# Sliding-window attention and a gated convolution FFN on one core: loading q and k through GpSimd's DMA queue with a cast on the way

## The chip, the core and the metric

The kernel runs on one core of a Trainium2 chip. The core has five engines that run side by side, each in its own instruction order: TensorE (PE, matrix products into PSUM), VectorE (DVE), ScalarE (ACT), GpSimd (POOL) and SyncE (SP, which here only issues transfers). Sixteen DMA engines move data between HBM and the on-chip memory SBUF; an issuing engine hands them work through its queue. The metric is the device time of one execution in microseconds. The kernel before took 213.82 us (median of 3 runs, 212.24 to 214.0).

## The reference, cut to what matters

Shapes: q, k and v are (8, 8, 576, 64) in fp32, that is batch, heads, sequence and head size; w_in is 512 x 1024, conv_w is 3 x 1024 and w_out is 1024 x 512.

```python
scores = q @ k.T / 8                            # per batch and head
scores = where(abs(i - j) <= 32, scores, -1e9)  # window of 32 to both sides
attn   = softmax(scores)
x      = concat_heads(attn @ v)                 # (8, 576, 512)
h      = maximum(x @ w_in, 0)                   # (8, 576, 1024)
conv   = conv_w[0]*h[s-1] + conv_w[1]*h[s] + conv_w[2]*h[s+1]
out    = (h * sigmoid(conv)) @ w_out            # (8, 576, 512)
```

The output is fp32. The kernel works in bf16 between the products.

## The kernel before, in words

**The order is written out by hand or by a planner.** The string `ORDER` (line 15) lists 869 steps as short words. A loop at line 654 calls one function per word, and each engine keeps exactly that order: an instruction that waits holds back all that stands behind it on its engine. `lq,1,0` is "load q of batch 1, head group 0"; a letter at the end names the engine (`a` ACT, `d` DVE, `p` POOL), and `@5` a PSUM bank. Since all instructions go through one helper (line 164), the profile gives line 164 for nearly all of them, and they are told apart by their tiles.

**Attention.** A batch has two units of four heads (G = 0, 1). For each unit, q and k (4 heads x 576 rows x 256 bytes, 576 KiB each) are loaded in fp32 into a staging tile `st` (`lq`, `lk`, line 194, SP's queue), cast to bf16 into `qb` by ACT or POOL (`cq`, `ck`, line 202), and transposed in blocks by DVE into `qT`, `kT` (`tq`, `tk`, line 206). A partition of `st` holds 18 consecutive rows of a head. For batch 0 each load, cast and transpose is made in two parts, which are the first nine and the last nine of the 18 rows of every partition, so a part is spread over the whole sequence and both are needed for any score.

Scores are made in two halves of the sequence (`sc`: h = 0 has the 64-row tiles 0 to 3, h = 1 the tiles 4 to 8; the keys of a tile reach 32 rows to both sides, so the first half needs q rows up to 256 and k rows up to 288), then the exponential (`ex`, ACT), the band mask (`mk`, DVE or POOL), the product with v and the row sums (`av`, PE), and the division (`nr`, DVE). v comes in five blocks of 128 rows per batch (`lv`, SP, 256-byte pieces) into `vst`, and is cast into `ve` (`cv`) and, shifted by 64 rows, into `vo` (`vo` by POOL from `vst` or by DVE from `ve`; `vd` copies it by DMA). The result x is transposed by PE and ACT (`xp`, `xe`) or by a DMA (`xt`).

**FFN.** Two batches together are cut into three chunks of 384 rows; the first two chunks are halved, which gives 14 pieces. For a piece, `ph` multiplies by w_in (PE, 256 channels at a time), `re` applies the relu (ACT), the convolution runs in one of several ways (`pc`, `tp`: `P` full diagonal matrices on PE, `A` and `D` quarter-array diagonal matrices on PE, `X` on ACT and DVE, `G` on POOL), `th` is the tanh that stands for the sigmoid (ACT), `ga` the gating (DVE), `py` multiplies by w_out (PE), `ye` moves it out of PSUM (ACT or DVE) and `st` stores it (SP). w_in and w_out come in four quarters of 512 KiB each (`li`, `lo`, SP's queue), and are cast by ACT or POOL (`ci`, `co`).

In the order before, SP issues at first the eight parts of q and k of batch 0, the five blocks of v, then k of unit (1,0), two quarters of w_in, q of (1,0), the two other quarters, and so on.

Of the kernel before, what the change touches and what calls it, by code (L numbers as in the profile page):

```python
# [10 lines left out]
U32 = mybir.dt.uint32  # L11
# [4 lines left out]
lk,0,0,0 lq,0,0,0 s3 s1 lq,0,0,1 lk,0,1,1 s2 lk,0,1,0 lk,0,0,1 cw@5 lq,0,1,1 lq,0,1,0 cc lv,0,2 dg,1,a dg,0,d lv,0,1  # L16
dg,2,d cq,0,0,0,a cq,0,0,1,p dg,7,a ck,0,1,1,p dg,4,a s4 tq,0,0,1 dg,5,a tk,0,1,1 ck,0,0,0,p dg,3,a s5 tq,0,0,0 s0
ck,0,1,0,a s7 tk,0,0,0 lv,0,3 ck,0,0,1,p tk,0,0,1 cq,0,1,1,a tk,0,1,0 sc,0,0,1@4 tq,0,1,1 cq,0,1,0,p sc,0,0,0@0
ex,0,0,1 lv,0,4 tq,0,1,0 cv,0,2,p lv,0,0 ex,0,0,0 mk,0,0,1,d sc,0,1,1@4 lk,1,0 ex,0,1,1 cv,0,1,p li,1 vo,0,1,d li,3
sc,0,1,0@4 mk,0,0,0,d lq,1,0 cv,0,3,a li,0 mk,0,1,1,d li,2 cv,0,4,a vo,0,2,d vo,0,3,d cv,0,0,a lq,1,1 ex,0,1,0  # L20
vo,0,0,d lk,1,1 av,0,0,0@0 mk,0,1,0,d lv,1,2 ck,1,0,a nr,0,0,0 av,0,1,0@3 nr,0,1,0 av,0,0,1@0 ci,1,a xp,0,1@6 nr,0,0,1
dg,6,a xp,0,0@2 xe,0,1,a ci,3,p av,0,1,1@4 xe,0,0,a nr,0,1,1 ph,0,3@3 lv,1,1 cq,1,0,p tk,1,0 xp,0,2@7 re,0,3 xp,0,4@5
xp,0,3@4 xe,0,2,a ph,0,1@0 xe,0,3,a tq,1,0 pc,0,3,P@6 ci,0,p re,0,1 ph,1,3@4 th,0,3,P xe,0,4,a ga,0,3,P sc,1,0,0@0
re,1,3 ph,0,0@5 ci,2,p ex,1,0,0 lv,1,0 pc,1,3,P@7 re,0,0 ph,2,0@4 mk,1,0,0,d th,1,3,P cq,1,1,p sc,1,0,1@0 ph,2,2@5
ex,1,0,1 ph,2,3@6 tq,1,1 re,2,2 ck,1,1,p lv,1,4 ph,2,1@3 ga,1,3,P ph,1,0@5 re,2,1 lv,1,3 tk,1,1 cv,1,2,p re,2,0
ph,1,1@0 re,1,0 re,1,1 mk,1,0,1,d lo,1 sc,1,1,0@1 cv,1,1,p lo,2 pc,0,1,P@5 ex,1,1,0 ph,0,2@7 cv,1,0,p vo,1,1,d re,2,3
sc,1,1,1@0 re,0,2 ph,1,2@4 vo,1,0,d ex,1,1,1 mk,1,1,0,d lv,2,1 av,1,0,0@6 lo,0 re,1,2 nr,1,0,0 cv,1,3,p av,1,1,0@0
lk,2,1 cv,1,4,a pc,1,0,P@2 lo,3 nr,1,1,0 pc,1,2,P@4 vo,1,3,p th,1,0,P lv,2,0 pc,0,0,P@7 th,0,1,P ga,1,0,P th,1,2,P
xp,1,0@3 mk,1,1,1,d xp,1,1@6 co,1,p xe,1,0,a pc,1,1,P@1 lq,2,1 xe,1,1,a ga,1,2,P pc,0,2,P@2 lk,2,0 ga,0,1,P pc,2,0,X@0
ph,3,2@3 vo,1,2,p th,1,1,P tp,2,0,X ph,3,0@4 re,3,2 th,0,2,P ph,3,1@6 re,3,0 lv,2,2 pc,3,2,G ga,0,2,P pc,2,3,P@5  # L30
th,0,0,P ga,1,1,P re,3,1 av,1,0,1@3 co,0,a ga,0,0,P av,1,1,1@1 nr,1,0,1 pc,2,2,P@6 lq,2,0 co,2,a pc,2,1,P@7 ck,2,1,p
nr,1,1,1 lv,2,3 ph,3,3@3 th,2,0,X th,2,3,P pc,3,0,P@4 re,3,3 co,3,p ga,2,3,P xp,1,4@1 th,2,1,P xp,1,3@2 pc,3,1,P@3
th,3,0,P ga,2,1,P cv,2,0,p pc,3,3,P@5 xe,1,4,a ga,2,0,X th,2,2,P xp,1,2@1 cv,2,1,p th,3,1,P py,0,1@7 ga,2,2,P vo,2,0,p
ga,3,1,P cq,2,1,a s6 tk,2,1 lv,2,4 py,0,2@6 tp,3,2,G xe,1,2,a tq,2,1 th,3,3,P xe,1,3,a lq,3,0 ga,3,0,P lk,3,0
sc,2,1,0@0 ga,3,3,P ck,2,0,p py,1,0@4 ex,2,1,0 ye,0,1,d cv,2,2,p th,3,2,G@5 lk,3,1 tk,2,0 ye,0,2,a vo,2,1,p sc,2,1,1@0
lv,3,0 cq,2,0,a ga,3,2,G ph,4,3@6 ye,1,0,d ex,2,1,1 lv,3,1 tq,2,0 cv,2,3,p py,0,0@4 vo,2,2,p re,4,3 mk,2,1,0,d lk,4,0
cv,2,4,a mk,2,1,1,d sc,2,0,1@0 ye,0,0,a vo,2,3,p av,2,1,0@6 ex,2,0,1 ph,4,2@4 nr,2,1,0 st,0,0 mk,2,0,1,d sc,2,0,0@0
# [24 lines left out]
st,5,1 tk,6,0 th,8,2,A ph,9,0@2 mk,5,0,1,d re,9,1 ga,8,2,A av,5,1,1@4 re,9,0 av,5,0,1@0 nr,5,1,1 pc,9,1,D@6 cq,6,1,a
# [24 lines left out]
def kernel(  # L87
# [22 lines left out]
    PAD = 32  # L110
# [71 lines left out]
    def slot(y, b, G):  # L182
        return 2 * unit(b, G) + y
# [507 lines left out]
```

## Time and profile before

| | |
|---|---|
| time, median of 3 runs | 213.82 us (212.24 to 214.0) |
| time of the profiled execution | 214.61 us |
| its span, first to last instruction | 212.9 us |
| busy: PE, DVE, ACT, POOL | 188.9, 178.5, 173.0, 147.7 us |
| DMA: bytes, mean rate over the span | 46.90 MB, 220 GB/s |
| mean granted TensorE clock | 0.998 |

A busy share is a mean over the whole span, and stages differ, so the tables by stage and the chain of work that ended last say more than the totals. In the groups by shape, a row gives the engine, the operation, output<-input by tile names, the shapes, the count, then the busy time in us, the mean ns of one, and the idle time of the engine ahead of them with what ended it. "DMA share" is the mean busy share of the 16 DMA engines; it can read a little over 1.

### The profile page before, as it was taken

The page shows a single profiled execution, that of the slowest core. Times are in us where ns is not written, and L with a number is a line of the kernel's source. Part 1 is how long each engine was busy: PE and PEld are TensorE (multiplying, and loading weights), DVE is VectorE, ACT ScalarE, POOL GpSimd, SP SyncE. Part 2 cuts the span into 40 slices and gives each one's busy share as a digit, 9 for nine tenths or more (in the row PEclk, how much of TensorE's full clock was granted, in tenths as well). Part 3 has the DMA queues.
Part 4 walks back from the last instruction along what each step waited for, and adds up shares of the span by engine and source line. Part 5 has one row for each costly group of instructions (what it writes and reads, how often), then busy time and mean ns, then how long its engine had stood idle before and what let it go on. Part 6 is the DMA issues. An engine that isn't in the chain of part 4 may idle for free.

```text
span 212.9 us, 7087 instructions
## 1 busy us (share of the span) xinstructions
PE 188.9 (89%) x2936; PEld 113.4 (53%) x2936; DVE 178.5 (84%) x297; ACT 173.0 (81%) x265; POOL 147.7 (69%) x177
## 2 busy tenths in 40 slices
PE   1035899999999799999999999999899997999994
PEld 0034899986566355644464554544555553545443
DVE  4689839999999999798999779898899487889860
ACT  2987778998899799789999699887989797759911
POOL 2630686379999569999799999497723979855700
PEclk9999999999999999999999999999999999999999
DMA  5999999999896794899999899979985664132225
GB/s 171 333 202 345 390 246 304 353 327 283 243 262 177 193 316 144 261 299 229 251 280 157 209 280 233 309 248 183 271 202 130 89 153 127 29 86 99 98 102 197
DMA packets 66165, 46.90 MB, mean 220 GB/s; under 512 B 53180, under 2 KB 55508, under 8 KB 66132
## 3 DMA queue, kind: packets, MB, share of 16 engines
q1 hardware_dynamic: 66096, 46.43, 83.0%
q8 instruction: 23, 0.38, 0.8%
q14 instruction: 10, 0.08, 0.2%
q10 hardware_dynamic: 36, 0.01, 0.1%
HBM read 32.52 MB, written 9.44 MB: 197 GB/s over the span
## 4 chain that ended last, share of the span: by engine, by line
PE 64%; DVE 13%; ACT 7%; SPq 6%; DMA 5%; issue 3%; ACTq 0%; DVEq 0%
PE PS L164 64%; SPq L164 6%; DVE gT L164 3%; DMA xT<-in_moe_w_in_dram 3%; DVE attn L164 2%; DVE xn L164 2%; DVE qT L164 2%; DVE PS L164 2%; ACT PS L164 2%; DMA xT<-xn 2%; ACT hT L164 1%; ACT attn L164 1%; ACT y L164 1%; ACT xT L164 1%; DVE rec L164 1%
## 5 line engine op out<-in xcount | busy, mean ns | idle before, releaser
L164 PE MATMUL PS<-xT,w_in_sb 128*128 128x385 bf16 (+3 forms) x448 | 70.7, 309 | 3.0 <-ACT y L164 1.3
L164 PE MATMUL PS<-w_out_sb,gT 128*128 128x512 bf16 (+1 forms) x296 | 66.7, 374 | 0.0
L164 DVE SCALAR_TENSOR_TENSOR gT<-PS,hT 128x384 bf16<-128x384 f32 (+2 forms) x82 | 52.6, 650 | 6.0 <-ACT PS L164 4.9
L164 PEld LDWEIGHTS <-w_in_sb 128*128 128x128 bf16 x448 | 41.4, 100 | 25.8 <-issue 5.6
L164 ACT ACTIVATE hT<-PS 128x770 bf16<-128x770 f32 (+3 forms) x56 | 39.9, 721 | 11.9 <-PE PS L164 9.5
L164 PEld LDWEIGHTS <-gT 128*128 128x128 bf16 x296 | 27.6, 98 | 30.2 <-issue 1.2
L164 ACT ACTIVATE attn<-PS 128x1280 bf16<-128x1280 f32 (+1 forms) x32 | 36.0, 1132 | 4.6 <-PE PS L164 4.1
L164 POOL TENSOR_TENSOR zg<-zg,tap 128x768 f32<-128x768 f32 (+1 forms) x18 | 31.8, 1764 | 1.5
L164 ACT ACTIVATE PS<-PS 128x768 f32<-128x768 f32 (+1 forms) x47 | 30.0, 652 | 3.0 <-PE PS L164 2.2
L164 PE MATMUL PS<-hT,diag_w 64*64 64x384 bf16 (+2 forms) x354 | 27.5, 311 | 0.1
L164 DVE TENSOR_TENSOR xn<-PS,rec 128x512 bf16<-128x512 f32 (+1 forms) x32 | 26.4, 824 | 1.1
L164 PE MATMUL PS<-qT,kT 32*128 32x64 bf16 x1152 | 15.3, 195 | 11.5 <-DVE kT L164 7.9
L164 POOL TENSOR_SCALAR ve<-vst 128x512 bf16<-128x512 f32 x24 | 16.8, 708 | 12.4 <-DMA vst<-in_v_dram 11.9
L164 DVE TENSOR_TENSOR attn<-attn,mask 128x1280 bf16<-128x1280 bf16 (+1 forms) x24 | 22.9, 959 | 2.1 <-ACT attn L164 1.9
L164 POOL TENSOR_SCALAR vo<-vst 64x512 bf16<-64x512 f32 x32 | 22.7, 708 | 2.5
L164 POOL TENSOR_SCALAR_AFFINE_SELECT attn<-attn 64x1024 bf16<-64x1024 bf16 (+1 forms) x16 | 19.7, 1234 | 6.7 <-ACT attn L164 6.0
L164 DVE STREAM_TRANSPOSE qT<-qb 128x576 uint32<-128x576 uint32 (+1 forms) x18 | 20.2, 1128 | 4.1 <-POOL qb L164 2.1
L164 POOL TENSOR_SCALAR qb<-st 128x1152 bf16<-128x1152 f32 (+1 forms) x18 | 18.9, 1054 | 6.7 <-DMA st<-in_q_dram 5.6
L164 PEld LDWEIGHTS <-kT 32*128 32x128 bf16 x1152 | 11.9, 96 | 21.2 <-issue 9.6
L164 ACT CAST qb<-st 128x1152 bf16<-128x1152 f32 (+1 forms) x18 | 19.1, 1073 | 2.0 <-DMA st<-in_q_dram 1.2
L164 POOL TENSOR_SCALAR tap<-hT,conv_w_sb 128x384 f32<-128x384 bf16 (+1 forms) x36 | 20.1, 571 | 0.9
L164 DVE STREAM_TRANSPOSE kT<-qb 128x576 uint32<-128x576 uint32 (+1 forms) x18 | 19.9, 1124 | 0.9 <-PE PS L164 0.8
(47 smaller groups left out, 195.7 us busy)
## 6 DMA issues: line engine op xcount, KB each, us to landing
out_dram<-y SPq DMA_DIRECT2D x35, 256.0 KB, 4.1
st<-in_k_dram SPq DMA_DIRECT2D x14, 576.0 KB, 6.2
st<-in_q_dram SPq DMA_DIRECT2D x14, 576.0 KB, 5.8
vst<-in_v_dram SPq DMA_DIRECT2D x24, 256.0 KB, 6.6
vst<-in_v_dram SPq DMA_DIRECT2D x16, 192.0 KB, 5.5
st<-in_k_dram SPq DMA_DIRECT2D x4, 288.0 KB, 5.3
st<-in_q_dram SPq DMA_DIRECT2D x4, 288.0 KB, 4.9
vo<-ve SPq DMA_DIRECT2D x8, 130.0 KB, 4.2
```

The source lines that it names most:

```text
L164: return lambda *args, **kwargs: tc.keep_in_program_order(do(*args, **kwargs))
```

## The change

- New steps `gq`, `gk` issue loads of q and k from GpSimd's queue straight into the bf16 tile `qb`; the transfer casts. They replace load and cast of all of batch 0 (eight loads, in parts) and of 22 of the 28 later loads (whole). The six others, q and k of unit (1,0), k of (3,0), k of (4,1) and k of (7,0) and (7,1), stay with SP and their casts with ACT (2) and POOL (4).
- The parts of batch 0 are now stretches of the sequence: q rows 0 to 255 and 256 to 575, k rows 0 to 287 and 288 to 575. The source of a part is 4 heads x 32 pieces of 8 to 10 rows.
- There are 5 tiles `st` instead of 6 and 6 tiles `qb` instead of 4.
- The whole order is new. SP now begins with the blocks of v, then two quarters of w_in, q and k of unit (1,0), and the two other quarters. Beside that, 5 mask products move from POOL to DVE, 7 evictions `ye` from DVE to ACT, 7 casts of v from POOL to ACT, 4 `vo` from DVE to POOL, 2 casts of w_out from ACT to POOL; one block of x is transposed by PE instead of by a DMA; of the convolutions, 15 instead of 19 are of kind `P`, and none of these is full-width (before: 5), 9 instead of 7 `A` and 15 instead of 13 `D`. Functions `gi`, `go` are added and not called.

The start of the order, and the functions:

```diff
-lk,0,0,0 lq,0,0,0 s3 s1 lq,0,0,1 lk,0,1,1 s2 lk,0,1,0 lk,0,0,1 cw@5 lq,0,1,1 lq,0,1,0 cc lv,0,2 dg,1,a dg,0,d lv,0,1
...
+gk,0,0,0 s5 s4 tk,0,0,0 s3 lv,0,1 lv,0,2 gq,0,0,0 lv,0,4 s1 lv,0,0 cw@1 gk,0,1,0 s0 lv,0,3 gq,0,1,0 cc s2 gq,0,0,1
+cv,0,2,a tq,0,0,0 gk,0,0,1 cv,0,1,a li,0 s7 sc,0,0,0@0 dg,5,a vo,0,1,p li,1 ex,0,0,0 tk,0,1,0 lq,1,0 lk,1,0 gk,0,1,1
+cv,0,0,a tq,0,1,0 li,2 gq,0,1,1 mk,0,0,0,d sc,0,1,0@0 li,3 vo,0,0,p ex,0,1,0 tq,0,0,1 dg,0,a mk,0,1,0,d cv,0,3,p
+cv,0,4,a tk,0,0,1 av,0,1,0@4 dg,3,a av,0,0,0@6 vo,0,3,p dg,1,a nr,0,1,0 lv,1,1 sc,0,0,1@0 nr,0,0,0 ex,0,0,1 vo,0,2,p
+tk,0,1,1 xp,0,0@7 tq,0,1,1 xp,0,1@6 xe,0,0,a ci,0,p mk,0,0,1,d xe,0,1,a sc,0,1,1@2 ex,0,1,1 gk,1,1 lv,1,0 av,0,0,1@0
+ci,1,a mk,0,1,1,d ph,0,0@5 nr,0,0,1 cq,1,0,p av,0,1,1@6 re,0,0 dg,2,a ph,0,1@3 nr,0,1,1 gq,1,1 re,0,1 ck,1,0,p tq,1,0
+xp,0,3@2 xp,0,2@6 xe,0,3,a pc,0,1,P@0 xe,0,2,a tk,1,0 xp,0,4@7 xe,0,4,a ph,1,1@1 ci,2,p tk,1,1 sc,1,0,1@2 re,1,1
...
-    NST, NQB, NQT, NAT, NY = 6, 4, 3, 4, 4
+    NST, NQB, NQT, NAT, NY = 5, 6, 3, 4, 4
...
+    def part_of(y, part):
+        if not part:
+            return 0, RP
+        first = (256, 288)[y] // 32
+        return (0, first) if part[0] == 0 else (32 * first, RP - first)
+
+    def columns(t, t0, g):
+        return t[:, 2 * t0:2 * t0 + D * g]
+
+    def rows(y, b, G, *part):
+        t0, g = part_of(y, part)
+        src = (q, k)[y][b, 4 * G:4 * G + 4, t0:t0 + 32 * g, :]
+        heads = [[S * D, 4], [g * D, 32]] if part else [[g * D, 128]]
+        return bass.AP(src.tensor, src.offset, heads + [[1, g * D]])
+
+    def load_qk(y, b, G):
+        sync.dma_start(st_[slot(y, b, G) % NST], rows(y, b, G))
+
+    def fetch_qk(y, b, G, *part):
+        gpsimd.dma_start(columns(qb_[slot(y, b, G) % NQB], *part_of(y, part)), rows(y, b, G, *part))
+
+    def cast_qk(y, b, G, e):
+        copy(e, qb_[slot(y, b, G) % NQB], st_[slot(y, b, G) % NST])
+
+    def turn_qk(y, b, G, *part):
+        t0, g = part_of(y, part)
+        src = columns(qb_[slot(y, b, G) % NQB], t0, g).bitcast(U32).rearrange("p (g d) -> p g d", g=g)
+        to = qT_[unit(b, G) % NQT] if y == 0 else kT_[unit(b, G) % NQT][:, PAD:PAD + S, :]
+        to = to[:, t0:t0 + 32 * g, :].rearrange("p s e -> p (s e)").bitcast(U32)
+        vector.transpose(to.rearrange("p (x g) -> p g x", g=g), src)
...
+        gq=lambda *a: fetch_qk(0, *a), gk=lambda *a: fetch_qk(1, *a),
```

More of the change, by code (lines that the diff above doesn't have):

```diff
@@ L21 @@
[L21 to L25, printed above, removed]
```

167 lines of the change are left out of this document (71 added, 96 removed).

## The prediction

> **What bounds the kernel now.** I read the page's summary first, then the table of stages, then the chain of waits in order of time, then the groups by shape.
>
> ```profile
> span 212.9 us, 7087 instructions
> PE 188.9 (89%) x2936; PEld 113.4 (53%) x2936; DVE 178.5 (84%) x297; ACT 173.0 (81%) x265; POOL 147.7 (69%) x177
> PE 64%; DVE 13%; ACT 7%; SPq 6%; DMA 5%; issue 3%; ACTq 0%; DVEq 0%
> ```
>
> TensorE is busy for 188.9 of 212.9 us and owns 64% of the chain that ended last. So 24.0 us is idle time of PE, and the question is where it lies.
>
> ```profile
> core 0: us, PE busy (x) PEld busy (x) DVE busy (x) ACT busy (x) POOL busy (x), PEclk, DMA share, GB/s
> 0.00:2.00 2.00, 0.00 (x0) 0.00 (x0) 0.57 (x8) 0.00 (x0) 0.71 (x6) 1.00 0.13 12
> 2.00:11.00 9.00, 0.59 (x2) 0.50 (x2) 5.16 (x19) 6.92 (x19) 4.11 (x8) 1.00 0.96 305
> 11.00:16.00 5.00, 2.13 (x133) 1.92 (x137) 4.46 (x8) 4.16 (x5) 1.92 (x3) 1.00 0.95 200
> 16.00:23.60 7.60, 4.48 (x116) 3.84 (x104) 6.66 (x17) 6.30 (x11) 1.05 (x1) 1.00 1.01 354
> 23.60:32.00 8.40, 8.38 (x142) 7.73 (x142) 5.07 (x6) 5.27 (x11) 6.84 (x7) 1.00 1.11 302
> 32.00:53.00 21.00, 20.40 (x344) 17.53 (x342) 20.00 (x36) 19.49 (x39) 14.54 (x22) 1.00 1.12 316
> 53.00:138.00 85.00, 83.59 (x1356) 45.00 (x1356) 77.83 (x114) 75.04 (x101) 73.01 (x83) 1.00 0.97 240
> 138.00:181.00 43.00, 40.52 (x655) 21.93 (x650) 35.76 (x57) 36.43 (x52) 30.95 (x34) 1.00 0.76 177
> 181.00:202.00 21.00, 21.00 (x189) 10.84 (x184) 18.92 (x33) 17.26 (x29) 14.56 (x17) 1.00 0.25 79
> 202.00:213.00 11.00, 7.85 (x45) 4.12 (x42) 4.08 (x6) 2.08 (x4) 0.00 (x0) 0.96 0.38 145
> ```
>
> Before 23.6 us PE is busy for 0.59+2.13+4.48 = 7.2 us, idle for 16.4. From 32 to 202 it is idle for only 0.60+1.41+2.48 = 4.5 us in 170, and at the end for 3.15. From 23.6 on, PE's own work sets the pace; what can be won is in the start. There the DMA share is 0.95 to 1.01 from 2 us on: the first 23.6 us are bound by transfers.
>
> ```profile
> 13.72 6.94 DMA xT<-in_moe_w_in_dram
> ...
> 20.69 1.05 ACT w_in_sb L164
> ...
> 23.62 11.51 PE PS L164 x170
> ```
>
> The chain says the same: a quarter of w_in lands at 20.66, ACT casts it, and the first FFN matmul runs at 23.62.
>
> **The change part by part.** The rows that carry its costs:
>
> ```profile
> L164 PE MATMUL PS<-hT,diag_w 64*64 64x384 bf16 x240 | 13.3, 330 | 0.0
> L164 PE MATMUL PS<-hT,diag_w 128*128 128x192 bf16 x84 | 8.8, 251 | 0.0
> L164 PE MATMUL PS<-hT,diag_w 128*128 128x384 bf16 x30 | 5.6, 326 | 0.1
> L164 POOL TENSOR_SCALAR vo<-vst 64x512 bf16<-64x512 f32 x32 | 22.7, 708 | 2.5
> L164 POOL TENSOR_SCALAR ve<-vst 128x512 bf16<-128x512 f32 x24 | 16.8, 708 | 12.4 <-DMA vst<-in_v_dram 11.9
> L164 POOL TENSOR_SCALAR qb<-st 128x1152 bf16<-128x1152 f32 x13 | 15.6, 1200 | 1.6 <-DMA st<-in_q_dram 0.9 <-DMA st<-in_k_dram 0.3
> L164 ACT CAST qb<-st 128x1152 bf16<-128x1152 f32 x15 | 17.2, 1156 | 2.0 <-DMA st<-in_q_dram 1.2 <-DMA st<-in_k_dram 0.8
> L164 DVE COPY vo<-ve 64x520 bf16<-64x520 bf16 x16 | 5.8, 362 | 0.2
> L164 ACT CAST ve<-vst 128x512 bf16<-128x512 f32 x16 | 9.8, 620 | 0.2 <-DMA vst<-in_v_dram 0.2
> L164 ACT COPY y<-PS 128x512 f32<-128x512 f32 x23 | 13.2, 586 | 6.8 <-PE PS L164 6.3 <-DMA out_dram<-y 0.4
> L164 POOL TENSOR_SCALAR_AFFINE_SELECT attn<-attn 64x1024 bf16<-64x1024 bf16 (+1 forms) x16 | 19.7, 1234 | 6.7 <-ACT attn L164 6.0
> L164 POOL MEMSET vst<- 32x512 f32 x2 | 1.0, 518 | 0.1
> L164 POOL TENSOR_SCALAR w_in_sb<-hT 128x1024 bf16<-128x1024 f32 x1 | 1.1, 1053 | 8.1 <-DMA hT<-in_moe_w_in_dram 8.1
> L164 DVE STREAM_TRANSPOSE kT<-qb 128x288 uint32<-128x288 uint32 x4 | 2.7, 708 | 0.1
> L164 SPq DMA_DIRECT2D st<-in_k_dram x18: 328/500/1056, 0.8 to 148.0; - x18
> L164 SPq DMA_DIRECT2D vst<-in_v_dram x40: 367/540/4158, 5.2 to 168.1; - x40
> DMA to landing us min/median/max: 2.9/5.8/10.6
> ```
>
> *Price of a GpSimd issue, e.* No row has one. SP issues the same q, k loads in 0.33 to 1.06 us, median 0.50, and a v load in up to 4.16: those are the ends. I take 0.9, about twice SP's median, since POOL needs 708 ns for a half of vo that DVE copies in 362. Below nothing I exclude: the issue is an added instruction. The Trainium skill ("DMA: Bandwidth & Descriptors", Specifications) gives about 1 us to the first byte on GpSimd's path against 0.6 on SP's; with 1.0 the sum below ends 0.8 us later.
>
> *The transfers of the start.* Before, SP moved in this order: q, k of batch 0 (eight loads of 288 KiB, 2.36 MB), v (1.18 MB), k of one unit of batch 1 (0.59), the w_in quarter that the chain waits for (0.52). At the stage rates that is 2.0 + 2.36/0.305 + 1.18/0.200 + (0.59+0.52)/0.354 = 2.0+7.7+5.9+3.1 = 18.7 us, 2.0 below the 20.66 at which it landed; I add that 2.0 as the landing. After, q, k go by GpSimd's queue and SP holds v, then two w_in quarters, then q, k of batch 1. Both queues draw on the same engines, whose share is already full, so I let them add: 2.0+7.7+5.9 = 15.6 for q, k and v together, and the first quarter 1.5 later, 17.1, landed by 19.1. I assume that a cast on the way moves source bytes at the rate of a plain load. From above: only half the bytes are written, up to 3.9 us less. From below: half the rate, 7.7 us more.
>
> *POOL's chain at the start*, in its order: eight issues; identity and mask, for which I allow 0.8 (the first 2 us hold 0.71 of POOL work); zero rows 1.0; four vo steps of 2 x 0.708; one v cast 0.71; the w_in cast 1.05: 9.2 us without the issues, 16.4 with 8 x 0.9, so from 0.8 done by 17.2 when nothing is late. Something is: the last v block comes with the end of q, k, v at 15.6, and behind it stand cv 0.71, two vo 2.83 and ci 1.05, so 20.2. PE's first FFN product stands there: 20.2 against 23.62.
>
> *DVE's chain* starts when the first part lands (0.8 and the least landing of 2.9, so about 4). All DVE work before 23.6 us is 16.9 by the stage table, with eight halves of vo that POOL now makes (2.9); the eight part transposes (0.71 each) and what stands between them can be no more than the other 14.0, so the last is done by 18: hidden, with 2 us to spare at least. A part is now a stretch of the sequence, so the first half's scores need only part 0. The new wait here is DVE's mask set-up behind the first transpose; POOL's mask step and its fifth issue queue behind that, and POOL comes to it at 0.8 + 4 x 0.9 + 1.3 = 5.7 anyway, after the transpose's 4.7.
>
> *Unit (1,0)* stays with SP and is late next. Its k is behind 2.36+1.18+1.05+1.18 MB: 2.0+7.7+5.9+3.0+3.3 = 21.9. Its casts stand on POOL behind ci, with an issue ahead of each (0.9+1.2+0.9+1.2), so 24.4, a transpose of 1.25, and PE's scores at 25.7. Two w_in casts queue behind (26.5). PE reaches these scores after three FFN products, the transposes of x and one convolution, exactly what stands ahead of the same scores before:
>
> ```profile
> 23.62 1.45 PE L164 MATMUL PS<-xT,w_in_sb 128*128 128x193 bf16 x8 [0.62 <-ACT xT L164]
> ...
> 28.81 0.42 PE L164 MATMUL PS<-qT,kT 32*128 32x64 bf16 x32
> ```
>
> 28.81-23.62 = 5.2 us, so 25.4 against 25.7. The start is worth 28.81-25.7 = **-3.1 us**. Bounds: -5 (cast at a better rate, e = 0.5) to +6 (below).
>
> *Conversions.* ACT and POOL lose 18 casts each and keep 2 and 4, 16.8 and about 14 us; ACT takes 7 v casts (620 ns) and 7 y evictions (586 ns), POOL 4 vo steps from DVE, DVE 5 mask products from POOL. POOL ends at 147.7-14.1+5.7-5.0+2.1-12.3 = 124 us plus 30 issues, 151 with e = 0.9. Neither sets the end, so the gain is nothing directly; PE is the cover.
>
> *Convolutions.* Five full-width pieces on diagonal matmuls (5.6/5 = 1.12 us of PE) become four on quarter tiles (13.3/20 = 0.67) and one more half piece (0.63): -2.3 us of PE. One more transpose of x (four products, against six in a half piece of 0.63) gives up to 0.5 back. DVE pays with two or three shorter gates in place of one, so I count half of the 1.8: **-0.9**.
>
> *Middle.* PE is idle for 4.5 us between 32 and 202. Lighter ACT may take some; a load that lands at 10.6 instead of the median 5.8 gives 4.8 back, and POOL's order now holds loads between its conversions: if one waits for a qb slot, the vo, cv and convolution taps behind it wait, and with them PE. Slots are six for four per batch, so I expect them free. **0**, from -4 to +9.
>
> Sum: -3.1-0.9 = -4.0: span 208.9. The profiled execution took 214.61 us with 212.9 of span, 0.8 above the median 213.82; on the median, **209.8 us**.
>
> **Rivals.**
> *A, given back (chance 0.20, about 213).* PE starts earlier, but batch 1's loads, now on two queues, come no earlier: the DMA share stays at 1.1 to 53 us, and a middle worse by 3 takes the rest. For it: the full share; against: only 0.6 us of idle PE from 32 to 53.
>
> *B, POOL's issues (0.22, 219.4).* POOL's 9.2 us and 8e, from 0.8 on, must fit before 23.62: with e over 1.7 POOL's w_in cast ends later than the start of before. At e = 2.2 it ends at 27.6, +4.0; POOL's total is 124+66 = 190, as much as PE, and in-order conversions cost perhaps 2.5 more: 213.8+4.0+2.5-0.9 = 219.4. For it: v loads that took SP 4.16. Against: SP's median of 0.50.
>
> *C, few engines for the parts (0.06, 219.4).* Their source has 4 heads outermost. If a part runs on four of 16 engines, it moves at 354/4 = 88 GB/s, 3.3 us a part. On rotating groups the first lands 2.4 later, which DVE's 2 us nearly cover. On the same four, all eight need 2.36/0.088 = 26.8 us: PE starts at about 30.1, +6.5, and 213.8+6.5-0.9 = 219.4. The Trainium skill ("DMA: Bandwidth & Descriptors", Why a DMA increments its semaphore by 16 and not by 1) states that the engines used are the largest number up to 16 that divides the slowest dimension of both sides, here 4, with rotating groups on GpSimd's path; it also notes direct copies there that take all 16. No row of before has such a load.
>
> *D, the cast is slow (0.06, 226).* At half rate q, k take 15.4 us: the start goes +4.3 against before; 22 loads add 1.67 us of all engines each, 37 in all, where the share is near 1. A quarter of that uncovered gives 213.8+4.3+9-0.9 = 226.
>
> *That it brings more (0.08, 205).* Start -5, middle -3.
>
> **How the numbers follow.** Forecast 0.38, from 207 to 211.6. About 1% (2.1 us) is what can be told from no change. Faster: 0.38+0.08 = 0.46. Within 1%: A, 0.20. Slower: B, C, D, 0.34. The range runs from 205.5, leaving out half of the last rival, to 221.5, leaving out D and the worse part of B: 0.82 held.
>
> **What would show it.** In the changed kernel PE's first product of xT with w_in starts near 20 us (right), or after 23.6 (wrong, then the row just before names POOL or a landing). The distance of POOL's early instructions gives e: about 0.9. The landing of q, k on GpSimd's queue beside 5.8 us, and the GB/s from 2 to 16 us, show a slow cast or few engines (below 200). PE's idle time from 32 to 202 stays near 4.5. POOL's total is near 150. The prediction fails if e exceeds 1.7, if the cast lowers the rate, or if PE meets late q, k after 53 us.

## The result and the profile after

The changed kernel takes **228.68 us** (median of 4 runs, 227.02 to 229.18) against 213.33 for the kernel before beside it: a ratio of 1.0711, 95% interval 1.0634 to 1.0789. The prediction was 209.8, from 205.5 to 221.5, and faster. The profiled execution took 229.13 us. Medians here are over all runs, while the ratios leave out executions more than 1.5% above the fastest of their kernel, so that differences read from the two can part by a few us.

The page of the changed kernel: span, busy times, queues (packets, MB, share of 16 engines), and the chain by engine.

```profile
span 227.4 us, 7115 instructions
PE 190.8 (84%) x2964; PEld 114.8 (50%) x2964; DVE 178.4 (78%) x294; ACT 165.9 (73%) x263; POOL 144.5 (64%) x186
q1 hardware_dynamic: 61232, 30.96, 58.7%
q0 software_dynamic: 7392, 7.68, 24.1%
PE 43%; DMA 18%; DVE 13%; POOL 9%; ACT 7%; issue 6%; SPq 3%; POOLq 0%; ACTq 0%; DVEq 0%
```

PE has about the work it had (190.8 us against 188.9), and 36.6 us of idle time against 24.0. Transfers own 18% of the chain; they owned 5%. The same stages as in the prediction show where.

```profile
core 0: us, PE busy (x) PEld busy (x) DVE busy (x) ACT busy (x) POOL busy (x), PEclk, DMA share, GB/s
2.00:11.00 9.00, 0.05 (x1) 0.05 (x1) 1.50 (x11) 1.92 (x3) 3.71 (x8) 1.00 1.03 175
16.00:23.60 7.60, 0.14 (x6) 0.14 (x8) 1.27 (x2) 2.94 (x10) 5.06 (x8) 1.00 1.15 282
23.60:32.00 8.40, 5.52 (x152) 4.56 (x150) 5.74 (x9) 4.48 (x5) 6.55 (x7) 1.00 1.24 209
32.00:53.00 21.00, 18.72 (x339) 16.70 (x338) 18.52 (x25) 14.60 (x29) 12.27 (x17) 0.92 0.90 208
53.00:138.00 85.00, 80.68 (x1329) 46.90 (x1326) 76.85 (x124) 69.33 (x108) 57.23 (x74) 1.00 0.96 170
138.00:181.00 43.00, 40.53 (x684) 22.21 (x683) 37.04 (x55) 33.41 (x49) 27.71 (x32) 1.00 0.94 190
```

From 16 to 32 us PE is busy for 5.66 us where it was busy for 12.86; with the stages ahead of them PE has done 8.1 us less by 32 us. From 32 to 202 it is idle for 2.28 + 4.32 + 2.47 = 9.1 us where it was 4.5. (GB/s counts the bytes written, and a casting load writes half of what it reads: alone, the same load read 77 GB/s with the cast and 152 without in e1 below. So GB/s reads lower here.)

The order of time on POOL, DVE and PE, from the timeline (start, duration, instruction, idle time before it and its cause):

```profile
5.17 0.67 POOL L162 DMA_DIRECT2D qb<-in_q_dram  x1
11.10 0.54 POOL L162 TENSOR_SCALAR_AFFINE_SELECT mask<-mask 128x64 bf16<-128x64 bf16 x2 [5.26 <-DVE mask L162]
11.59 0.69 POOL L162 DMA_DIRECT2D qb<-in_q_dram  x1
...
14.96 0.67 POOL L162 DMA_DIRECT2D qb<-in_q_dram  x1
```

```profile
8.95 0.69 DVE L162 STREAM_TRANSPOSE kT<-qb 128x288 uint32<-128x288 uint32 x1 [7.71 <-DMA qb<-in_k_dram]
...
10.85 0.11 DVE L162 MEMSET mask<- 128x64 bf16 x1
...
22.14 0.74 DVE L162 STREAM_TRANSPOSE qT<-qb 128x320 uint32<-128x320 uint32 x1 [7.29 <-DMA qb<-in_q_dram]
...
27.91 0.76 DVE L162 STREAM_TRANSPOSE qT<-qb 128x320 uint32<-128x320 uint32 x1 [0.61 <-DMA qb<-in_q_dram]
```

```profile
30.78 1.45 PE L162 MATMUL PS<-xT,w_in_sb 128*128 128x193 bf16 x8 [0.25 <-ACT attn L162]
...
38.20 0.48 PE L162 MATMUL PS<-qT,kT 32*128 32x64 bf16 x40
```

This is a ring of waits that the new order ties. DVE's mask set-up stands behind its first transpose; that waits for the first part of k, which lands at 8.9 us; POOL's mask step waits for DVE's until 11.10; and the last four part loads stand behind it in POOL's order, so the last is issued at 14.96, lands at 27.9, and PE's first FFN product runs at 30.78 instead of 23.62.

### The profile page after: what moved, and what is told of

It is laid out like the page before. It is cut to its first block, busy times and chain, and to the rows that moved or that the text cites. A ratio compares the mean times of both kernels' runs of the same rounds, so it can differ in the third digit from the quotient of the medians.

```text
span 227.4 us, 7115 instructions
## 1 busy us (share of the span) xinstructions
PE 190.8 (84%) x2964; PEld 114.8 (50%) x2964; DVE 178.4 (78%) x294; ACT 165.9 (73%) x263; POOL 144.5 (64%) x186
## 3 DMA queue, kind: packets, MB, share of 16 engines
q0 software_dynamic: 7392, 7.68, 24.1%
## 4 chain that ended last, share of the span: by engine, by line
PE 43%; DMA 18%; DVE 13%; POOL 9%; ACT 7%; issue 6%; SPq 3%; POOLq 0%; ACTq 0%; DVEq 0%
PE PS L162 43%; DMA qb<-in_k_dram 7%; DMA qb<-in_q_dram 6%; DVE attn L162 4%; POOL zg L162 3%; DVE gT L162 3%; DMA vst<-in_v_dram 3%; SPq L162 3%; DMA vo<-ve 2%; POOL tap L162 2%; ACT hT L162 2%; DVE xn L162 2%; ACT PS L162 2%; DVE qT L162 1%; DVE kT L162 1%
## 5 line engine op out<-in xcount | busy, mean ns | idle before, releaser
L162 ACT ACTIVATE attn<-PS 128x1024 bf16<-128x1024 f32 (+1 forms) x32 | 36.1, 1129 | 12.8 <-PE PS L162 12.7
L162 ACT ACTIVATE PS<-PS 128x384 f32<-128x384 f32 (+1 forms) x47 | 29.2, 629 | 11.5 <-PE PS L162 9.1
L162 POOL TENSOR_TENSOR zg<-zg,tap 128x768 f32<-128x768 f32 x18 | 33.0, 1834 | 1.5
L162 PE MATMUL PS<-hT,diag_w 64*64 64x384 bf16 (+1 forms) x378 | 26.3, 313 | 2.6 <-DVE gT L162 1.4
L162 DVE STREAM_TRANSPOSE qT<-qb 128x576 uint32<-128x576 uint32 (+2 forms) x18 | 20.2, 1122 | 8.8 <-DMA qb<-in_q_dram 8.8
L162 PE MATMUL PS<-ve,attn 128*64 128x65 bf16 x384 | 15.7, 203 | 10.4 <-DVE attn L162 9.5
L162 POOL TENSOR_SCALAR zg<-hT,conv_w_sb 128x384 f32<-128x384 bf16 x18 | 10.8, 609 | 21.3 <-ACT hT L162 21.2
L162 ACT COPY y<-PS 128x512 f32<-128x512 f32 (+1 forms) x31 | 17.5, 580 | 7.6 <-PE PS L162 7.0
L162 PEld LDWEIGHTS <-attn 128*64 128x64 bf16 x640 | 13.2, 117 | 19.2 <-DVE attn L162 10.8
L162 POOL TENSOR_SCALAR tap<-hT,conv_w_sb 128x384 f32<-128x384 bf16 x36 | 22.4, 633 | 0.7
L162 PEld LDWEIGHTS <-diag_w 64*64 64x64 bf16 (+1 forms) x378 | 15.5, 105 | 9.1 <-issue 5.2
```

The source lines that it names most:

```text
L162: return lambda *args, **kwargs: tc.keep_in_program_order(do(*args, **kwargs))
```

## The experiments

Times are medians; the number behind each is the ratio to runs of the kernel before on the same chip, with its 95% interval.

**e1_prices: what a load costs by itself.** A kernel of its own, with only loads in it; the part has the source access pattern of the change (4 heads x 32 pieces), the whole load that of the kernel before (128 rows).

```diff
+heads = [[S * D, 4], [g * D, 32]] if part else [[g * D, 128]]
+for e, part, cast in ((sync, 0, 0), (gpsimd, 0, 0), (gpsimd, 0, 1), (sync, 1, 0), (gpsimd, 1, 0), (gpsimd, 1, 1)):
+    load(e, 0, part, cast)
+    clear()
```

> This kernel computes nothing of the reference; it only loads q, k and v in fixed patterns and stores zeros, so that a load's landing can be read with nothing beside it. One load at a time, first whole (576 KiB) and then a part of 288 rows (288 KiB): by SP plain, by GpSimd plain, by GpSimd with the cast; then four at a time; then v's five blocks alone, and beside four loads of another queue. If parts run on few engines (theory K), a lone part has a DMA share of at most 0.25 and lands later than a lone whole load of twice its size, from SP as from GpSimd, with the cast or without. If the cast is slow (theory C), four whole loads with the cast take 1.5 to 2 times as long as four plain ones from GpSimd. If v's small pieces take the engines from the other queue (theory Q), four parts beside v land 3 us or more later than without v, whichever queue they come from.

Its timeline: the issue, then DVE's first write to the tile, which waits for the landing. First three whole loads (SP plain, GpSimd plain, GpSimd cast), then two parts of half the bytes (SP plain, GpSimd cast).

```profile
4.26 0.39 SPq L42 DMA_DIRECT2D ld<-in_q_dram  x1
7.84 0.15 DVE L42 MEMSET ld<- 128x1 f32 x4 [3.55 <-DMA ld<-in_q_dram]
...
8.36 0.67 POOL L42 DMA_DIRECT2D ld<-in_k_dram  x1 [7.91 <-DVE ld L42]
12.24 0.15 DVE L42 MEMSET ld<- 128x1 f32 x4 [4.11 <-DMA ld<-in_k_dram]
...
12.76 0.53 POOL L42 DMA_DIRECT2D ld<-in_q_dram  x1 [3.73 <-DVE ld L42]
16.61 0.15 DVE L42 MEMSET ld<- 128x1 f32 x4 [4.08 <-DMA ld<-in_q_dram]
...
16.84 0.71 SPq L42 DMA_DIRECT2D ld<-in_k_dram  x1
22.90 0.15 DVE L42 MEMSET ld<- 128x1 f32 x4 [6.00 <-DMA ld<-in_k_dram]
...
29.81 0.69 POOL L42 DMA_DIRECT2D ld<-in_k_dram  x1 [5.69 <-DVE ld L42]
35.56 0.14 DVE L42 MEMSET ld<- 128x1 f32 x4 [5.96 <-DMA ld<-in_k_dram]
```

```profile
12.76:16.61 3.85, 0.00 (x1) 0.53 (x1) 1.00 0.52 77
29.81:35.56 5.75, 0.00 (x0) 0.69 (x1) 1.00 0.22 27
```

A whole load takes 3.6 us by SP, 3.9 plain and 3.85 cast by GpSimd: neither the queue nor the cast makes it much slower. A part has half the bytes and takes 5.75 to 6.06, whoever issues it, at a share of 0.22 of the 16 engines against 0.52 (windows of the two casting loads, DMA share next to last). The Trainium skill ("DMA: Bandwidth & Descriptors", Why a DMA increments its semaphore by 16 and not by 1) gives four engines for such a pattern, a quarter; the row agrees. Four casting loads at a time took 9.0 us whole and 10.3 in parts, for half the bytes. The same run has v's five blocks on SP's queue, first alone and then beside four casting parts; this write of DVE waits for v:

```profile
80.62 0.06 DVE L42 MEMSET vst<- 128x5 f32 x1 [7.32 <-DMA vst<-in_v_dram]
...
92.70 0.06 DVE L42 MEMSET vst<- 128x5 f32 x1 [0.80 <-DMA vst<-in_v_dram]
```

v takes 7.5 us alone (from 73.1) and 12.0 beside the parts (from 80.7), while the parts take 10.8 instead of 10.3. So v does not make GpSimd's parts late, as the expectation's theory Q had it; it is SP's transfers that lose beside a second queue.

**e2_mask_first: the mask wait alone.**

```diff
-gk,0,0,0 s5 s4 tk,0,0,0 ... s1 lv,0,0
+gk,0,0,0 s1 s5 s4 tk,0,0,0 ... lv,0,0
```

> The changed kernel with the identity and mask set-up (s1) ahead of DVE's first transposes, so that GpSimd's mask step, and with it the fifth to eighth load of batch 0, no longer wait for the first load's landing. Theory M (that wait, 5.3 us of POOL, is the start's loss): the fifth issue comes at about 6 us instead of 11.6, the last part lands at 22 to 23 instead of 27.9, PE's first FFN product comes 4 to 5 us earlier, and the time falls to about 223 to 225. Theories K and Q (the transfers themselves are late): the issues come earlier but the landings hardly, the first part still lands at about 9, and the time falls by less than 2 us.

```profile
6.41 0.69 POOL L162 DMA_DIRECT2D qb<-in_q_dram  x1
...
9.78 0.67 POOL L162 DMA_DIRECT2D qb<-in_q_dram  x1
```

221.24 us, ratio 1.0341 (1.027 to 1.0412): 7.4 below the changed kernel. The first part is still transposed at 8.92, but the last is issued at 9.78, not 14.96, and PE's first FFN product stands at 25.45. One word at the wrong place of the order is worth 7.4 us.

**e3_whole: batch 0 in four whole loads.**

```diff
-gk,0,0,0 ... gq,0,0,0 ... gk,0,1,0 ... gq,0,1,0 ... gq,0,0,1 ... tq,0,0,0 gk,0,0,1
+gk,0,0 ... gq,0,0 ... gk,0,1 ... gq,0,1 ... tq,0,0
```

> The changed kernel with batch 0's q and k in four whole loads (source of 128 equal pieces) instead of eight parts (4 heads outermost); they are issued where the first parts were, ahead of the mask step. Theory K: whole loads land at about 8 to 9 us each, no later than the parts of half their size did, all four by 12 to 14, and the time falls by 6 us or more, to 222 or less. Theory M alone would give about the same as putting the mask first, some 224. Theory Q: four whole loads land no earlier than 16 to 20, since the same bytes share the engines with v, and the time stays above 224.

221.78 us, 1.0367 (1.0293 to 1.044). The first load is transposed at 7.03 and all four by 14.3; the first FFN product stands at 22.42, ahead of the kernel before. That is 6.9 us below the changed kernel, but it is not the price of the few engines alone. With four loads in place of eight parts, all of them stand ahead of the mask step:

```profile
4.75 0.53 POOL L161 DMA_DIRECT2D qb<-in_q_dram  x1
9.75 0.54 POOL L161 TENSOR_SCALAR_AFFINE_SELECT mask<-mask 128x64 bf16<-128x64 bf16 x2 [4.47 <-DVE mask L161]
```

POOL still waits 4.47 us for the mask, and no load of batch 0 waits with it. So e3 breaks the ring too, and holds most of e2's repair; e12 below parts the two. The start is repaired, and yet the kernel is 3.7% slower than before.

**e4_later_on_sp and e5_before_later_gp: the later loads the other way round.**

```diff
-... gk,2,1 ... tk,2,1          (e4, the changed order)
+... lk,2,1 ... ck,2,1,p tk,2,1
...
-... lk,2,1 ... ck,2,1,p ... tk,2,1  (e5, the order before)
+... gk,2,1 ... tk,2,1
```

> The changed kernel with the 22 later loads of q and k back on SP's queue in the same places of the order, plain, and their casts by ACT and POOL in turn just ahead of each transpose; batch 0 stays as changed. Theory C (cast loads cost the engines more, and the middle stalls on them): PE's idle time from 32 to 138 us falls from 6.6 towards the 2.0 of the kernel before, and the time falls by 3 to 5 us, to 224 to 226. If the later loads cost nothing, the 22 casts come back onto ACT and POOL in an order that was not made for them, and the time is 229 or more.

> The kernel before, its order and its start kept, with the same 22 later loads issued by GpSimd with the cast at the places where SP issued them, their casts on ACT and POOL dropped, and six qb tiles. If GpSimd's queue in itself costs the middle (the two queues share the engines and SP's v, transposes and stores land later), PE's idle time from 32 to 138 us rises from 2 to 5 us or more and the time is 216 or more. If the middle of the changed kernel lost by its new order and not by the queue, this one is no slower than before: 211 to 214.

e4 took 245.22 (1.1501, 1.1436 to 1.1566): DVE's transposes wait 15.9 us for the casts that ACT has got back, in an order not made for them, so this says nothing of the queue. e5 took 224.35 (1.0477, 1.038 to 1.0574): with the start, order and parts of the kernel before, 22 loads by GpSimd cost 10 us by the ratio, although 22 casts fell away. The row of its middle:

```profile
53.00:138.00 85.00, 78.05 (x1224) 41.49 (x1235) 71.26 (x105) 59.04 (x81) 68.91 (x88) 0.98 0.88 169
```

PE is busy for 78.05 of these 85 us, against 83.59 before (11 of its matmul records are missing here, so the loss is somewhat smaller than it looks).

**e6_no_later, e7_hoist, e8_before_start_gp.** e6 is e3 without the 22 later loads; e7 is e3 with the mask step first, eight `qb` tiles and the later loads up to 40 steps earlier; e8 is the kernel before with only batch 0 by GpSimd, in four whole loads.

```diff
-gk,1,1 gq,1,1 gq,2,1 gk,2,1 ...     (e6: all 22 gone)
...
-... 40 words ... gk,2,1             (e7)
+gk,2,1 ... 40 words ...
...
-lk,0,0,0 lq,0,0,0 ... cq,0,0,0,a    (e8)
+gk,0,0 gq,0,0 gk,0,1 gq,0,1 ...
```

> The kernel with batch 0 in whole loads, with the 22 later loads by GpSimd left out, so that the transposes of those units read what lies in qb (scores of batches 1 to 7 are mostly of old q and k); all else of the order stays. If the later loads cost the middle, PE's idle time from 32 to 138 us falls from 8.1 us to about 2 and the time from 221.8 to 215 or less. If the new order itself is the cause, the idle time stays at 6 or more and the time is 219 to 222.

> Whole loads of batch 0, the mask set-up ahead of DVE's first transpose, eight qb tiles (and three st), and each later GpSimd load up to 40 steps earlier in the order, not ahead of the transpose that frees its tile. If the later loads come too late because their issue stands behind POOL's work, the middle's idle time falls to 3 to 4 us and the time to 216 to 218. If not, the time stays at 220 to 222.

> The kernel before with only the start changed: q and k of batch 0 come in four whole loads by GpSimd with the cast, ahead of all else on its queue, the eight casts on ACT and POOL are dropped, and the four transposes are whole; SP begins with v; all later loads stay with SP. By the prices measured alone, four whole loads beside v land within 10 to 11 us of the first issue, as late as before, and w_in's first quarter lands at 18 to 20 instead of 20.7. If the idea of the start is sound, PE's first FFN product comes 1 to 2 us ahead of 23.6 and the time is 211 to 213; if sharing the engines takes it all, 213 to 215.

e6 took 213.12 (0.9977, 0.9928 to 1.0026): the later loads cost 8.7 us by the medians and 8.3 by the ratios, and the new order as such is not what makes the kernel slow. Nor does it make it fast: with 30 of 36 casts gone, and 22 loads with them, the time is that of the kernel before. e7 took 220.47 (1.0303, 1.018 to 1.0427): issuing earlier hardly helps. e8 took 212.60 (1.0009, 0.9966 to 1.0051): its scores of batch 1 start at 26.79, 2.0 ahead of the kernel before, and the gain is not seen at the end.

**e9 to e11: what of the later loads costs.** All are e3 with another form of the 22 loads (e9 brings 64 of the 1152 elements of a partition; e11 has three `st` tiles instead of five).

```diff
+            dst, src = dst[:, 0:64], bass.AP(src.tensor, src.offset, [[RP * D, 128], [1, 64]])  # e9_tiny
...
+        dst = qb_[slot(y, b, G) % NQB] if b == 0 else spare_[slot(y, b, G) % 3]                 # e10_unread
+        gpsimd.dma_start(dst, rows(y, b, G, *part))
...
+            sync.dma_start(spare_[slot(y, b, G) % 3], rows(y, b, G, *part))                     # e11_unread_sp, fp32
```

> The kernel of e3_whole (batch 0 in four whole loads, 221.8 us), but each of the 22 later loads by GpSimd's queue brings only 64 of the 1152 elements of each partition; issue, slot waits, order and every wait for a landing stay. It leaves work out: the scores of batches 1 to 7 are mostly those of older q and k. Theory B, the bytes: with an eighteenth of them the 8.7 us between e3_whole and e6_no_later go, 213 to 215 us. Theory W, the issues on POOL and the waits of the order (a slot that is still read, POOL held behind it): they stay, 219 to 222 us. A share of each: between 215 and 219.

> The kernel of e3_whole, but the 22 later loads go, whole and cast, at their old places into three spare tiles that nothing reads; the transposes take what is in the old tiles. It leaves work out: the scores of batches 1 to 7 are those of old q and k. If the price is that a consumer waits for its own late q or k (theory L), it goes: 213 to 215 us. If the price is indirect (theory S, the loads take DMA engines from v, vo, x transposes and y and POOL's time for the issues), it stays: 219 to 222 us.

> As e10_unread, but the 22 unread loads are plain ones by SP's queue into three spare fp32 tiles, at the same places of the order: the same bytes read, twice the bytes written, no issue on POOL, and v, vo, x transposes and y queue behind them in one queue instead of sharing engines. Leaves the same work out. If bytes as such cost (theory S without regard to the queue), as e10_unread, within 2 us. If GpSimd's queue or its issues cost (theory G), nearer to e6_no_later's 213 than e10_unread is, 213 to 216.

e9 took 215.93 (1.0216, 1.0115 to 1.0317), e10 221.99 (1.0485, 1.0385 to 1.0585), e11 215.29 (1.0087, 1.0024 to 1.0149). Nothing reads the loads of e10 (only GpSimd itself waits, twice, 3.2 us in all, until an older load has landed in the same spare tile), and it is as slow as e3: **the price is not that a late q or k holds somebody up**. With an eighteenth of the bytes 3 (by the ratios) to 6 us (by the medians) of the 8.7 go; the rest stays though few bytes move. And the same bytes by SP's queue cost 2 (215.29 against 213.12). The clock is not the reason: runs with a mean granted clock of 1.0 took 220.02 and 221.28 us in e3, and 211.60 to 213.99 in e6. Where the price shows is in the landings of the eight shifts of v (`vo` from `ve`, SP's queue) and in the waits from 50 to 181 us. For e10:

```profile
DMA to landing us min/median/max: 2.3/4.8/7.3
```

```profile
POOL ve L162 <- DMA vst<-in_v_dram: 15.6, 3, 7.4
PEld L162 <- DMA vo<-ve: 4.4, 2, 2.3
PE PS L162 <- DMA vo<-ve: 4.1, 2, 2.1
```

For e11:

```profile
DMA to landing us min/median/max: 3.3/4.1/4.8
```

```profile
POOL ve L162 <- DMA vst<-in_v_dram: 7.7, 3, 3.3
```

With the second queue the slowest shift lands after 7.3 us instead of 4.8, and PE waits 4.1 us for two of them; in e11 no row has PE wait for a transfer in the middle. The DMA engines have no more to do. These are SP's queue in e6 and e11, then SP's and GpSimd's in e10:

```profile
q1 hardware_dynamic: 61232, 30.96, 57.6%
...
q1 hardware_dynamic: 64400, 43.94, 82.4%
...
q1 hardware_dynamic: 61232, 30.96, 58.3%
q0 software_dynamic: 3744, 7.67, 23.0%
```

By these shares, 22 loads take (82.4% of 210.9) - (57.6% of 213.2) = 51.0 us of all 16 engines in e11 over e6, and in e10 (span 222.0) 44.7 us on GpSimd's queue (less the 3.0% of 213.2 that it has in e6) and 6.6 us more on SP's, 51.3. Not all of the difference between e10 and e11 is the queue's. From 16 to 53 us PE is busy 30.1 us in e10 and 32.5 in e11, where two mask products of DVE take 4.22 us in all and 2.37 (e12 below shows why); from 53 to 202 us it is busy 141.5 and 146.7.

**e13 to e15: which queue.** e13 and e14 issue unread loads on ACT's queue, e14 with 64 elements only; e15 is e10 without the cast. All three have three `st` tiles, as e11.

```diff
+scalar.dma_start(spare_[slot(y, b, G) % 3], src)             # e13_unread_act
+scalar.dma_start(spare_[slot(y, b, G) % 3][:, 0:64], src)    # e14_tiny_act
+gpsimd.dma_start(spare_[slot(y, b, G) % 3], src)             # e15_unread_plain, fp32
```

> As e11_unread_sp (the 22 later loads plain, into spare tiles that nothing reads), but issued on ACT's queue: the same bytes, a second queue beside SP's, and not GpSimd's. Leaves the same work out as e10_unread. Theory R, any second queue shares the 16 engines with SP's transfers and makes those late: the shift of vo from ve lands in 5 us or more as in e10_unread (5.5; e11_unread_sp 4.1), and the time is e14_tiny_act's plus 4 to 7 us. Theory G, GpSimd's queue alone does it: landing near 4, and within 2 us of e14_tiny_act.

> The control of e13_unread_act: the same issues on ACT, with 64 of 1152 elements of each partition. Leaves the same work out. It has what the issues cost on ACT and no bytes to speak of: 213 to 218 us by either theory; vo's shift lands near 3.4 as in e9_tiny.

> As e10_unread by GpSimd's queue, but plain, fp32 into spare fp32 tiles, no cast. Leaves the same work out. If the cast on the way is what costs, near e11_unread_sp's 215; if the sharing or GpSimd's queue as such, near e10_unread, 219 to 223.

e15 took 221.73 (1.044, 1.0366 to 1.0515): the cast is not it. e14 took 213.43 (1.0064, 1.0019 to 1.0109). e13's four runs went from 222.28 to 232.49, too far apart for a ratio; the fastest is 8.85 above e14's median, more than the 4 to 7 expected. GpSimd's queue is not special: ACT's does the same or worse. The table has the kernels of e3's order and the two compared, by the slowest shift (the waits are PE's, for the shifts, from 50 to 181 us; e13's profile is that of its slowest run, 232.49 us):

```
                                22 later loads      slowest   PE waits
e13_unread_act                  ACT's queue         12.5 us   3.1 us
the changed kernel              GpSimd's            10.9      2.6
e10_unread                      GpSimd's             7.3      4.1
e15_unread_plain                GpSimd's, no cast    6.6      1.9
e3_whole                        GpSimd's             6.2      3.2
e6_no_later                     none                 5.1      0
e9_tiny                         GpSimd's, 1/18       4.9      0
e11_unread_sp                   SP's                 4.8      0
e14_tiny_act                    ACT's, 1/18          4.8      0
the kernel before               SP's                 4.5      0
```

The medians do not part the two groups (3.9 us in e3, 4.1 in e11), where I had expected it for e13; in this order the slowest and PE's waits do. It is no law of the shift: in other orders e8 has one of 6.0 us and e4 of 6.6 with the later loads on SP's queue, and in e5 (6.4) PE doesn't wait for it, though its middle is as dear. In e7 the slowest is 7.1 and PE waits 0.7 us, and the time is hardly lower than e3's. The Trainium skill ("DMA: Bandwidth & Descriptors", Queues, rings and completion order) says that an engine goes round the queues that have work, a packet at a time. The runs agree in that a second queue of either kind stretches SP's transfers; the turns themselves no run shows.

**e12, e16, e17: why the two repairs do not add.** e12 is e3 with the mask step first; e16 is e12 with the last mask product of batch 0 on POOL; e17 is e12 with four casts on ACT.

```diff
-gk,0,0 s5 s4 ... s1 ...                       (e12)
+gk,0,0 s1 s5 s4 ...
...
-mk,0,1,1,d                                    (e16)
+mk,0,1,1,p
...
-cq,1,0,p ck,1,0,p ci,2,p ci,3,p               (e17)
+cq,1,0,a ck,1,0,a ci,2,a ci,3,a
```

> The kernel of e3_whole with DVE's mask set-up ahead of its first transposes, as in e2_mask_first: both repairs of the start, nothing else. If they add up where the start still sets the pace (first FFN product at 22.4 in e3_whole, 23.6 in the kernel before), some 1 to 3 us below e3_whole, 219 to 221 us; if after e3_whole the start is no longer what decides, 221 to 222. Faster than the kernel before by neither.

> The kernel of e12_whole_mask, with the band mask of batch 0's last half unit (the product that took 4.17 us on DVE) made by POOL, in its order ahead of batch 1's casts. Theory P, DVE's product and POOL's casts hold each other up, and that is why the two repairs do not add: PE's second FFN product at 25.5 to 26.5 in place of 27.86, the time 1 to 3 us below e12_whole_mask, 218.5 to 220.5. Rival, the start is no longer what decides: 221 to 222.

> The kernel of e12_whole_mask, with POOL's four casts beside that product (q and k of unit (1,0), two quarters of w_in) made by ACT. Theory P: the product takes 1.1 us or less again and the second FFN product comes at 25 to 26; what ACT loses (four casts of about 1.1 us) comes back behind, 218 to 222 us. Rival (the product is slow for another reason, its data or DVE itself): it stays near 4 us.

e12 took 221.67 (1.0379, 1.0221 to 1.0538; its four runs go from 218.41 to 223.30): 7.4 us and 6.9 us together give 7.0. The first reason is that they repair the same thing, since in e3 no load waits behind the mask. What the whole loads bring beside that is e12 against e2, both with the mask first: PE's first FFN product stands at 22.84 instead of 25.45, but the second at 27.86 instead of 28.29, and the times do not differ within their intervals. The 2.6 us are lost at one product of DVE, which takes 4.17 us in e12, 3.17 in e3 and 2.00 in e2 and the changed kernel. DVE's mask products in e12, and POOL beside them:

```profile
20.75 0.83 DVE L161 TENSOR_TENSOR attn<-attn,mask 128x1280 bf16<-128x1280 bf16 x1 [1.04 <-ACT attn L161]
22.83 4.17 DVE L161 TENSOR_TENSOR attn<-attn,mask 128x1280 bf16<-128x1280 bf16 x1 [1.25 <-ACT attn L161]
```

```profile
21.40 1.18 POOL L161 TENSOR_SCALAR qb<-st 128x1152 bf16<-128x1152 f32 x1
22.54 0.58 POOL L161 DMA_DIRECT2D qb<-in_q_dram  x1
23.14 1.16 POOL L161 TENSOR_SCALAR qb<-st 128x1152 bf16<-128x1152 f32 x1
24.27 1.05 POOL L161 TENSOR_SCALAR w_in_sb<-gT 128x1024 bf16<-128x1024 f32 x1
25.27 1.04 POOL L161 TENSOR_SCALAR w_in_sb<-hT 128x1024 bf16<-128x1024 f32 x1
```

The same instruction takes 0.83 us and, while POOL makes casts one after the other, 4.17: it ends at 27.00 where a row of casts has just ended at 26.31. e17 takes the casts away:

```profile
22.45 0.83 DVE L161 TENSOR_TENSOR attn<-attn,mask 128x1280 bf16<-128x1280 bf16 x1 [1.26 <-ACT attn L161]
```

It is 0.83 again, PE's second FFN product comes at 24.65 instead of 27.86, and e17 takes **216.62 us** (1.0239, 1.0161 to 1.0316), 5 below e12 by the medians, 3 by the ratios, and 4.9 below e16, which ran beside it; it is the best form of the change that still makes all of its loads. That product reads two tiles of SBUF; the Trainium skill ("SBUF — State Buffer", Who interferes with whom) states that such an instruction and a GpSimd one that reads SBUF hold each other up, and the rows agree: POOL's casts lose too, one of w_in takes 1.62 us instead of 1.04 in the changed kernel. e16 took 221.51 (1.0462, 1.0386 to 1.0538): POOL needs 2.84 us for the product and its casts come as much later, so PE's second FFN product, at 26.51, gains 1.4 and nothing is left at the end. So e16's time is that of its rival, though the wait it aimed at is shorter; for e17 the rival falls. By 53 us PE has been busy 2.7 us more in e17 than in e12 (32.5 us from 16 us on, against 29.8). The granted clock in that stretch is 0.92 in e12 and e16 and 1.00 in e17, but it is not what makes the 5 us: at mean clocks of 0.991 and 0.992 single runs took 220.27 (e12), 221.85 (e16) and 216.25 (e17).

**e18_vo_dve: the shift without a queue.** e3, with the shifts as copies by DVE.

```diff
-vd,4,0
+vo,4,0,d vo,4,1,d
```

> The kernel of e3_whole, with the four shifts of v by DMA (vo from ve on SP's queue, batches 4 to 6) made as copies by DVE in the same places (16 copies of 0.36 us). If the price of the second queue is paid at this transfer (PE's 3.2 us of waits for it in e3_whole): 218 to 219.5 us. If the next late transfer (v, stores, x) takes its place: 220.5 to 222.5.

227.09 (1.069, 1.0567 to 1.0812), worse than either expectation. DVE is busy for 189.6 us (180.1 in e3, where 5.8 more were counted on), and PE now waits for DVE's gates 5.8 us from 50 to 181 (1.0 in e3) where it waited 3.2 for the shift. So PE's wait was not lifted in this way; how much of the second queue's price is paid at the shift, and how much at v (POOL's wait for v falls from 15.6 us in e10 to 7.7 in e11), stays open.

## Why the prediction was wrong, point by point

**"The transfers of the start" failed, in two ways.** It let q and k move at the rate of plain whole loads, the first part landing at about 4. A part moves at a quarter of the engines: it takes 5.75 us alone, in the kernel 7.6, and the first transpose is at 8.95. Even a whole load, beside v, is transposed only at 7.03 (e3), so the few engines are 1.9 of the 5 us. They are rival C, to which I gave 0.06, with its place right and its price wrong: it put a part at 3.3 us and saw the delay "nearly covered" by DVE's 2 us on rotating groups. That its other case, all parts one after the other, put PE's start at 30.1, and 30.78 was measured, is luck: four parts overlap (10.3 us in e1), and the last was late because it was issued at 14.96. What the few engines cost by themselves is small, 2.6 us at the first FFN product and nothing clear at the end (e2 against e12). More costly was that eight parts left four loads behind the mask, where POOL waits hardly less with whole loads (4.47 us in e3, 5.26 here). With whole loads (e3) the first FFN product stands at 22.42; my 20.2 was still 2.2 too early, though POOL's chain had its w_in cast done at 20.4 (and at 21.6 in the changed kernel, 9 us ahead of PE's product: the sum followed the wrong chain). PE comes to that product only behind the last scores of batch 0 (20.34 in e3), which wait for mask, exponential and products in turn; I had asked when POOL and DVE are free, not how long that chain is.

**"DVE's chain" failed.** "The new wait here is DVE's mask set-up behind the first transpose; ... POOL comes to it at 5.7 anyway, after the transpose's 4.7." I had seen the wait and what stands behind it, and compared two numbers 1 us apart, one of which rested on the unmeasured landing. POOL comes to it at 5.84 and waits 5.26 us. e2: 7.4 us. A cover of 1 us behind a bound as wide as that landing was no cover.

**"Middle: 0, from -4 to +9" was mis-sized**: +8.7 by e3 against e6, inside its bounds, and by a cause that stood in no rival with that price, so that the bounds held by luck. I looked for a slot or a late q; e10 shows neither. Rival A named the full DMA share and two queues, but took them for a matter of batch 1 alone, worth 3.

**"Unit (1,0)" and the sum.** Batch 1's scores came at 38.20, not 25.7, and 7.4 us behind the first FFN product where 5.2 had been counted. Of the 15.35 us of the result, the two repairs of the start give 7.0 together, and the later loads 8.7 in the repaired kernel: 15.7.

**What was right.** *e*: taken as 0.9, it is 0.67 to 0.86 for a part and 0.53 to 0.61 for a whole load (0.73 where it is the kernel's first), so rival B falls; POOL's total is 144.5, predicted near 150 (ACT and POOL lose 16 and 14 casts, as the sums there have it, not 18 each). Rival D falls: a cast runs at the rate of the bytes it reads (3.85 us against 3.88 plain in e1). *Convolutions*: in the runs of the new order with all matmul records and a granted clock of 1.00 from 32 to 53 us (e9, e11, e17) PE is busy for 186.3 to 187.8 us against 188.9, so 1.1 to 2.6 less, where the sum had 0.9; in the changed kernel it is 190.8, with a clock of 0.92 there, and the runs don't tell how much of that is the clock. The sign that I had named for few engines was a poor one: GB/s was to be below 200 from 2 to 16 us, and it is 175 to 11 us and 346 from 11 to 16, while e3, without few engines, has 203 to 11 us.

## What to carry to other kernels

Count an instruction that waits for a landing as lasting as long as the worst landing, and put nothing behind it, on its engine or on those that wait for it, that issues the next loads. Bulk loads on a second queue were not free here, where the DMA share is near 1: the first queue's transfers got slower at their worst, and whoever waits for these pays, even if nobody reads the bulk. Two repairs of one wait don't add, so ask what each still leaves standing. Look at the pattern of a load (how many engines it runs on) before its bytes.

## What the runs showed of the hardware that was not expected

- Half the bytes can take 1.5 times as long: 5.75 us for 288 KiB in four heads, 3.85 for 576 KiB in 128 rows. GpSimd's queue had 7392 packets with eight parts and 3744 with four whole loads (e3) for the same bytes.
- Four parts by GpSimd overlap (10.3 us for all); four plain parts by ACT's queue, beside v, landed 3.4 to 3.7 us apart, the last 17.7 us after the first was issued.
- One DVE product beside POOL's casts took 4.17 us, without them 0.83.
- v's five blocks on SP's queue took 7.5 us alone and 12.0 beside four parts on GpSimd's queue.
- The granted clock from 32 to 53 us was 0.92 in the profiles of the changed kernel, e2, e4, e6, e7, e10, e12, e13, e15, e16 and e18, and 1.00 in those of the kernel before, e3, e5, e8, e9, e11, e14 and e17. The 0.92 is a mean: the clock is 0.50 for some 3.4 us (48.1 to 51.6 us in the changed kernel, 42.0 to 45.5 in e12), shortly after PE has stood mostly idle (busy for 1.3 of the 3 us to 48, and for 0.2 of the 2 us to 41). But e3, busy for 0.4 of the 2 us to 40, has no such spell, so what decides stays open.
